# Both overflow blocks of two expert layers behind one branch at the end, and the early rows' routing between the first layer's products

## The chip, the cores and the metric

The kernel runs on one core of a Trainium2 chip. The metric is the device time of one execution in microseconds (us), lower is better. An execution is timed from outside; the profiled one also has a span, from its first to its last instruction.

## What is computed

A chunked state-space attention gives `x` of shape (3072, 256). Two mixture-of-experts layers follow, each with 8 experts, one expert per row, and no limit on how many rows an expert may get:

```python
def _moe_ref(x, expert_emb, tau, w1, w2):
    ...
    logits = xn @ en.T / tau
    expert_idx = np.argmax(logits, axis=1)
    ...
    for e in range(E):
        mask = expert_idx == e
        ...
        h = np.maximum(x[mask] @ w1[e], 0.0)
        out[mask] = gate_w[mask, None] * (h @ w2[e])
    return out.astype(np.float32)

def reference(**kwargs):
    ...
    x = _moe_ref(x=x, **moe_kwargs)
    return _moe2_ref(x=x, **moe2_kwargs)
```

`_moe2_ref` is the same with `logits = x @ w_gate`. The weights are 256x1024 and 1024x256 per expert.

## The kernel before

**Stages.** The attention runs first and routes its rows by batches: GpSimd (POOL) scatters each row with indirect DMAs into a DRAM buffer `scr1`, in which every expert of the first layer has its own stretch (`route`, L144 to L229). The first layer takes the experts in turn: SyncE (SP) loads the expert's rows (`load_rows`, L274), TensorE (PE) transposes them (`x_split_k`, L284), multiplies by the first weights in eight column blocks (`mm1_f`, L299; tiles h0 to h7), then by the second (`mm2_steps`, L321; tiles y0 and y1). Weights and rows are split into a high and a low part, so each product is three matmuls. ScalarE (ACT) and VectorE (DVE) take each h tile out of PSUM (hh on ACT at L311, then hl on DVE at L312) and split the next expert's weights between (`wsplit`, L104: a cast on ACT at L120, a difference on DVE at L121). `finish1` (L395) routes the results into `scr2`, and the second layer reads them from there and scatters its results into `out` (`put_out`, L434).

**Capacities.** The main code of the first layer takes 432 rows of an expert (NMX). That of the second takes 384 rows and, behind one branch per expert (L1322), 256 more. The branch's condition is a count that every engine loads into a register (`values_load`, a TENSOR_LOAD at L1320). Rows past these capacities go through `rest` (L460): a register load of the largest count (L465), one branch over the whole block (L467), and inside it, for each expert, another load, another branch and a loop over 128 rows. `rest(0, ...)` stands before the first layer's first expert (L1220), `rest(1, ...)` before the second layer's (L1303). With these inputs neither block is entered.

**Early rows.** 162 rows of the first expert (NE0) are there after half of the batches; `early1` (L359) multiplies them during the attention, and tile names end in m0a. Their routing into `scr2` is the generator `prev` at L1223, which is run to its end (L1224) before the first expert's other 270 rows are transposed (L1226). `early_rows` and `mm1_early` do the same for 128 rows of the first two experts of the second layer (names n0a, n1a).

**Order.** The order of instructions on each engine is the order of the code (`manual_schedule`, L57); each engine runs its own in sequence. A generator's `yield` marks where other work may be put; `adv(1)` (L1229) runs `prev` by one such step after each h tile of the first layer.

**A skipped block.** On the skipped side of a branch each engine waits for what it still has in flight on the semaphores that the block would use and raises them as the block would have; on POOL this ends in an INC_SWDGE_SEM. After the last line every engine has a DRAIN and a barrier (L1398).

Of the kernel before, what the change touches and what calls it, by code (L numbers as in the profile page):

```python
# [9 lines left out]
F32 = mybir.dt.float32  # L10
F32R = mybir.dt.float32r
BF16 = mybir.dt.bfloat16
I32 = mybir.dt.int32
AF = mybir.ActivationFunctionType
ALU = mybir.AluOpType
AX = mybir.AxisListType
PSUM = bass.MemoryType.PSUM
# [12 lines left out]
R1 = NTOK + 384  # L30
R2 = NTOK + 512
# [5 lines left out]
def ssm_moe_moe_kernel(  # L37
# [44 lines left out]
    def wload0(raw):  # L82
        """weights of the first expert"""
        for which in range(2):
            w0.append(raw[:, which * KD * F:(which + 1) * KD * F])
            sp.dma_start(w0[which], wsrc[0][which][0])
            for k in range(2):
                wraw[2 * which + k] = w0[which][:, k * WP:(k + 1) * WP]
# [55 lines left out]
    def route(pn, nt, scale, vi, which, rows, scr, scr_rows, scats, psp, tag, lag=0, hole=None):  # L144
        """rows [pn,nt,272]: values and logits, id; vi [pn,nt,2] valid, invalid. To the experts' rows of scr."""
# [85 lines left out]
    def make_hole(which, n, ne, psp, name):  # L231
        """rows to leave out so that the next row of each of the first ne experts is its n-th or a later one"""
        pr = psp.tile([128, 512], F32, tag="c", name="hole" + name)
        pe.matmul(pr[:1, :ne], lhsT=ones[:, 0:1], rhs=cums[which][:, :ne], start=True, stop=True)
        t = const.tile([1, ne], F32, name="t" + name)
        dve.tensor_scalar(t, pr[:1, :ne], -1.0, float(n), op0=ALU.mult, op1=ALU.add)
        dve.tensor_scalar(holes[which][:, :ne], t, 0.0, None, op0=ALU.max)

    def counts(cum, hole, psp, name):
        """row 0: the eight counts; then their maximum"""  # L240
        pr = psp.tile([128, 512], F32, tag="c", name="cnt" + name)
        pe.matmul(pr[:1, :E], lhsT=ones[:, 0:1], rhs=cum[:], start=True, stop=hole is None)
# [103 lines left out]
    def begin1(xr, pn, nt, tag, rows=None):  # L346
        """ids; which rows hold a token"""
        if rows is None:
            rows = xpool.tile([128, 4, 272], F32, tag="rows2", name="rows2" + tag)
            va = rt.tile([128, NT, 2], F32, tag="va", name="va" + tag)  # L350
        else:
            rows, va = rows
        pool.tensor_copy(rows[:pn, :nt, 265:266], xr[:pn, :nt, 265:266])
        pool.tensor_scalar(va[:pn, :nt, 0:1], xr[:pn, :nt, 265:266], float(NTOK), None, op0=ALU.is_lt)
        pool.tensor_scalar(va[:pn, :nt, 1:2], xr[:pn, :nt, 265:266], float(NTOK), BIG,
                           op0=ALU.is_ge, op1=ALU.mult)
        return rows, va

    def early1():  # L359
        """rows for the first expert that are there after half of the batches"""  # L360
# [99 lines left out]
    def rest(m, cnt, done, scr, base, psp):  # L460
        """rows of any expert past the first `done`, 128 at a time"""
        why = "counts of tokens"
        with tc.tile_pool(name=f"rest{m}", bufs=1) as rp:
            top = NTOK + (NE if m else NE0)
            nmax = nc.values_load(cnt[0:1, E:E + 1], min_val=0, max_val=top,  # L465
                                  skip_runtime_bounds_check_because=why)
            with tc.If(nmax > done):  # L467
                for e in range(E):
                    n = nc.values_load(cnt[0:1, e:e + 1], min_val=0, max_val=top,
                                       skip_runtime_bounds_check_because=why)  # L470
                    with tc.If(n > done):
                        ws = []
                        for which in range(2):
                            w = rp.tile([128, KD * F], F32, tag=f"w{which}", name=f"rw{m}_{e}_{which}")
                            sp.dma_start(w, wsrc[m][which][e])
                            ws.append(w)
                        sp.dma_start(scr[ds(e * base + n, 128), :], zrow[:, 0, :])
                        with tc.For_i(done, n, 128) as i:
                            row = nc.s_assert_within(
                                i, 0, base - 128, skip_runtime_bounds_check_because=why)  # L480
                            rest_block(m, rp, psp, scr[ds(e * base + row, 128), :], ws, f"r{m}_{e}")

    def rest_block(m, rp, psp, src, ws, tag):
# [15 lines left out]
        if m == 0:  # L499
            yt = rp.tile([128, KD, 128], F32, tag="yt", name="yt" + tag)  # L500
            for dd in range(KD):
                p = psp.tile([128, 512], F32, tag="a", name=f"y{dd}{tag}")
                for f in range(KF):
                    o = f * D + dd * 128
                    pe.matmul(p[:, :128], lhsT=ws[1][:, o:o + 128], rhs=ht[:, f, :],
                              start=(f == 0), stop=(f == KF - 1))
                act.copy(yt[:, dd, :], p[:, :128])
            for _ in finish1(yt, xr, begin1(xr, 128, 1, tag), 128, 1, psp, None, tag):
                pass
        else:  # L510
            ids = out_rows(xr, 128, 1, tag)
            p = psp.tile([128, 512], F32, tag="a", name=f"o{tag}")
            for f in range(KF):
                pe.matmul(p[:, :D], lhsT=ht[:, f, :], rhs=ws[1][:, f * D:(f + 1) * D],
                          start=(f == 0), stop=(f == KF - 1))
            put_out(p, xr, ids, 128, 0, False, tag)

# [1 line left out]
    scats1 = []  # L519
    with ExitStack() as actx:  # L520
# [11 lines left out]
        def load_half(n):  # L532
            """B^T and C^T of half the chunks of a batch, all heads"""
# [10 lines left out]
        def expand_half(n, raw):  # L544
            """block diagonal over the two heads of a unit"""
# [50 lines left out]
        def cb_steps(b, k):  # L596
            """C B^T of chunks 2k, 2k+1 of all heads, times L"""
# [52 lines left out]
        def expand_x(q, xc, copy=dve.tensor_copy):  # L650
            """block diagonal over the two heads"""
# [9 lines left out]
        def dma_x(q):  # L661
            """the same without an engine"""
# [11 lines left out]
        def quad_p(q):  # L674
            """decays from the start of a chunk, on the partitions of its C"""
# [12 lines left out]
        def quad_c(q, r):  # L688
            """decayed C, block diagonal over the chunks of a group"""
# [9 lines left out]
        # chunk c of a quad: bank ((c - 1) // 4) % 3, slot (c - 1) % 4  # L699
# [58 lines left out]
        # token tiles of a batch in the order in which they become ready  # L758
# [41 lines left out]
        def run(gen, n=None):  # L800
            """advance gen by n steps (to its end if n is None)"""
# [33 lines left out]
        # idk[p, k] = [p mod 32 = k]; hm[p, h] = [p // 16 mod 2 = h]  # L835
# [14 lines left out]
        def a_part(lo, hi):  # L850
            """decays in parts hi (rows 0:32) + lo (rows 32:64), 0 at the start of a chunk"""
# [32 lines left out]
        def chunk_start():  # L884
            """decays from the start of a chunk; decays of whole chunks"""
# [17 lines left out]
            # on the partitions (4 heads, d)  # L903
# [271 lines left out]
    with ExitStack() as c1:  # L1175
# [44 lines left out]
        rest(0, cnt1, NMX, scr1, R1, psM)  # L1220
# [3 lines left out]
        for _ in prev:  # L1224
            pass
# [43 lines left out]
        # rows for the first experts of the second layer that are there already  # L1269
# [28 lines left out]
    N2, X2 = C2P * C2T, C2P * X2T  # L1298
    psM = ctx.enter_context(tc.tile_pool(name="psM2", bufs=2, space=PSUM))
    psX = ctx.enter_context(tc.tile_pool(name="psX", bufs=3, space=PSUM))  # L1300
    psH = ctx.enter_context(tc.tile_pool(name="psH2", bufs=3, space=PSUM))

    rest(1, cnt2, N2 + X2, scr2, R2, psM)  # L1303
    epool = ctx.enter_context(tc.tile_pool(name="epool", bufs=1))
    for e in range(E):
# [27 lines left out]
        xr, xs, nt = nxr, nxs, nnt  # L1333

# [5 lines left out]
def _layout(inputs):  # L1340
# [14 lines left out]
    # chunk c = 4 g + r + 1 at rows (r, h, n)  # L1355
# [46 lines left out]
```

## Time and profile before

| what | us |
|---|---|
| three executions | 504.42, 508.36, 508.38 |
| median | 508.36 |
| span of the profiled execution | 502.2 |
| median less span | 6.2 |
| PE busy in the span | 459.6 |

The page gives the profiled execution by its span alone; what lies around the span is taken as the 6.2 us of the last but one line. In the rows further down, PE is the matmuls and PEld the weight loads; a q behind an engine's name is its sequencer or queue, which executes register loads, branches and semaphore instructions, and these do not count as busy. PEclk is the granted clock of TensorE as a share of its full 2.4 GHz, so 0.50 is 1.2 GHz.

### The profile page before, as it was taken

To read this page: it belongs to the slowest core of one execution; us is meant where nothing else is said; L and a number is where in the kernel's file an instruction comes from. 1 tells how busy PE (TensorE), PEld (TensorE's weight loads), DVE (VectorE), ACT (ScalarE), POOL (GpSimd) and SP (SyncE) were. 2 spreads that over 40 slices of the span, in tenths; PEclk is the share of its full clock that TensorE was granted. 3 is DMA by queue.
4 is the path that set the end of the run, shared out by engine and by line. 5 is a ranking of instruction groups with operands and counts; after the bars stand their busy time and mean duration, and the time that the engine had idled before them with its cause. 6 is when DMAs were issued, how large, how long until landed. Compare 5 with 4: busy or idle time off the path is not lost.

```text
span 502.2 us, 8903 instructions
## 1 busy us (share of the span) xinstructions
PE 459.6 (92%) x3177; PEld 413.3 (82%) x3177; DVE 288.2 (57%) x681; ACT 240.6 (48%) x557; POOL 138.2 (28%) x210
## 2 busy tenths in 40 slices
PE   7969988888869999999999999969999999999992
PEld 3645656667769999999999999869999999999991
DVE  6786788777645836547373656723666357244330
ACT  5532454456535544637354455524566346344330
POOL 6334456165730031230303021411101210212011
PEclk9857999989879999999999999989999999999997
DMA  7265799995225534242443444260654564411000
GB/s 249 89 200 118 190 230 245 219 281 185 89 80 173 180 110 179 92 159 104 142 145 119 144 136 177 79 213 19 222 192 159 170 217 154 134 40 58 22 23 15
DMA packets 50226, 72.22 MB, mean 144 GB/s; under 512 B 23870, under 2 KB 36093, under 8 KB 49899
## 3 DMA queue, kind: packets, MB, share of 16 engines
q1 hardware_dynamic: 45595, 61.66, 40.8%
q0 software_dynamic: 4560, 9.70, 5.8%
q8 instruction: 34, 0.56, 0.5%
q14 instruction: 37, 0.30, 0.2%
HBM read 52.53 MB, written 19.74 MB: 144 GB/s over the span
## 4 chain that ended last, share of the span: by engine, by line
PE 34%; DMA 21%; issue 12%; POOL 2%; POOLq 1%; another core or an unknown queue 0%; DVE 0%; ACT 0%
DMA out_dram<-os0n,idsn 13%; PE y1m L330 7%; DMA out_dram<-os0n0a,idsn0a 7%; PE y0m L330 7%; PE h0m L308 2%; PE h1m L308 2%; PE h6m L308 2%; PE h2m L308 2%; PE h3m L308 2%; PE h5m L308 2%; PE h4m L308 2%; PE h7m L308 2%; POOL out_dram L437 1%; POOL scr L218 1%; PE rkm L197 1%
## 5 line engine op out<-in xcount | busy, mean ns | idle before, releaser
L218 POOL DMA_INDIRECT scr<-rows2m,idxm x31 | 31.5, 1017 | 126.6 <-DVE cum L215 104.1
L121 DVE TENSOR_TENSOR w0l<-raw,w0h 128x1024 fp32r<-128x1024 f32 x30 | 36.7, 1224 | 10.2 <-ACT w0h L120 10.2
L121 DVE TENSOR_TENSOR w1l<-raw,w1h 128x1024 fp32r<-128x1024 f32 x30 | 36.4, 1215 | 1.0 <-ACT w1h L120 1.0
L603 PE MATMUL cb<-cw,btt 128*128 128x256 f32 x96 | 33.1, 462 | 3.5 <-DVE mb L610 1.2
L437 POOL DMA_INDIRECT out_dram<-os0n,idsn x8 | 7.8, 971 | 88.8 <-ACT os0n L436 46.1
L218 POOL DMA_INDIRECT scr<-rows,idxa x24 | 26.1, 1086 | 22.0 <-DVE cum L215 12.3
L120 ACT CAST w1h<-raw 128x1024 fp32r<-128x1024 f32 x30 | 31.5, 1053 | 0.0
L580 DVE TENSOR_TENSOR_SCAN lt<-ab,ipat 128x512 f32<-128x512 f32 x24 | 29.2, 1216 | 3.5 <-PE ab L577 3.3
L120 ACT CAST w0h<-raw 128x1024 fp32r<-128x1024 f32 x30 | 31.1, 1041 | 0.0
L312 DVE SCALAR_TENSOR_TENSOR hln<-h0n,hhn 128x384 fp32r<-128x384 f32 (+1 forms) x8 | 4.2, 524 | 45.7 <-ACT hhn L311 45.7
L603 PEld LDWEIGHTS cb<-cw,btt 128*128 128x128 f32 x96 | 18.4, 219 | 11.2 <-issue 4.1
L610 DVE TENSOR_TENSOR mb<-cb,lt 128x256 f32<-128x256 f32 x48 | 18.0, 416 | 10.9 <-PE cb L603 10.7
L330 PE MATMUL y1m<-hhm,w1h 128*128 128x432 f32 (+1 forms) x64 | 23.0, 360 | 0.0
L330 PE MATMUL y0m<-hhm,w1h 128*128 128x432 f32 (+1 forms) x64 | 22.9, 358 | 0.0
L312 DVE SCALAR_TENSOR_TENSOR hlm<-h0m,hhm 128x432 fp32r<-128x432 f32 (+1 forms) x8 | 4.7, 586 | 31.5 <-ACT hhm L311 31.5
L330 PE MATMUL y0m<-hhm,w1l 128*128 128x432 f32 (+1 forms) x64 | 22.4, 350 | 0.0
L330 PE MATMUL y1m<-hhm,w1l 128*128 128x432 f32 (+1 forms) x64 | 22.3, 349 | 0.0
L330 PE MATMUL y0m<-hlm,w1h 128*128 128x432 f32 (+1 forms) x64 | 22.3, 348 | 0.0
L330 PE MATMUL y1m<-hlm,w1h 128*128 128x432 f32 (+1 forms) x64 | 22.3, 348 | 0.0
L704 PE MATMUL y<-mb,xbd 128*64 128x80 f32 x384 | 19.0, 246 | 2.4 <-DMA xbd<-in_xs__dram 2.0
L591 POOL TENSOR_TENSOR mb<-brt,lt 128x128 f32<-128x128 f32 x24 | 11.1, 462 | 36.8 <-DVE lt L580 30.2
L704 PEld LDWEIGHTS y<-mb,xbd 128*64 128x64 f32 x384 | 15.9, 144 | 6.0 <-issue 3.0
(603 smaller groups left out, 1552.4 us busy)
## 6 DMA issues: line engine op xcount, KB each, us to landing
raw<-in_m2w_dram SPq DMA_DIRECT2D x32, 512.0 KB
raw<-in_m1w_dram SPq DMA_DIRECT2D x28, 512.0 KB
scr<-zrow SPq DMA_DIRECT2D x8, 448.9 KB
scr<-zrow SPq DMA_DIRECT2D x8, 399.0 KB
xrm<-scr SPq DMA_DIRECT2D x7, 448.9 KB
xrn<-scr SPq DMA_DIRECT2D x6, 399.0 KB
xbd<-in_xs__dram SPq DMA_DIRECT2D x24, 96.0 KB
scr<-zrow SPq DMA_DIRECT2D x8, 266.0 KB
```

The source lines that it names most:

```text
L120: act.copy(hi[:, sl], raw)
L121: dve.tensor_tensor(lo[:, sl], raw, hi[:, sl].bitcast(F32), ALU.subtract)
L218: i = pool.indirect_dma_start(out=scr[:], out_offset=bass.IndirectOffsetOnAxis(ap=idx[:pn, t, :], axis=0), in_=rows[:, t, :W], in_offset=None,
L308: pe.matmul(p[:, :n], lhsT=w[:, o:o + 128], rhs=x[:, kd, :n], start=(k == 0), stop=(k == 5))
L312: dve.scalar_tensor_tensor(hl[:, f, :n], p[:, :n], 0.0, hh[:, f, :n].bitcast(F32), op0=ALU.max, op1=ALU.subtract,)
L330: pe.matmul(p[:, :n], lhsT=w[:, o:o + 128], rhs=h[:, f, :n], start=(k == 0), stop=(k == 3 * KF - 1))
L437: i = pool.indirect_dma_start(out=out, out_offset=bass.IndirectOffsetOnAxis(ap=ids[:pn, t, :], axis=0), in_=o[:pn], in_offset=None, bounds ...
L580: dve.tensor_tensor_scan(lts[b, g][:, 2 * v:2 * v + 2].rearrange("p u c i -> p (u c i)"), p, ipat[:].rearrange("p c i -> p (c i)"), 0.0, o ...
L591: pool.tensor_tensor(m[:, :, :, 64:80], brs[b][:, us_, 4 * g:4 * g + 4], lt[:, us_, :, CH - 1:CH].to_broadcast([128, 2, 4, NS]), ALU.mult,)
L603: pe.matmul(p[:, cc], lhsT=btt[:, c].rearrange("p h j -> p (h j)"), rhs=ctt[:, :, c * CH:(c + 1) * CH], start=True, stop=True)
L610: dve.tensor_tensor(mbs[2 * b + hq, g][:, :, o:o + 2, :64].rearrange("p u c i -> p c u i"), p[:, :, us_, :], lts[b, g][:, us_, o:o + 2, :] ...
L704: pe.matmul(yps[g][64 * hs:64 * hs + 64, r * 80:r * 80 + 80], lhsT=xts[hs][:, c, :], rhs=mbs[q, c // 4][:, hs, c % 4, :], start=(r == 0), ...
```

## The change

`rest` is taken out of both places and called once, after the second layer, with one branch for both layers' blocks. If it is entered, the first layer's block routes its rows into `scr2` past row 640 of each expert (`push_hole`), counts again, and the second layer's block follows; `scr2` gets 256 more rows per expert for this. The loop that ran the early rows' routing to its end before the first expert is gone, so that `adv(1)` runs it step by step between that expert's h tiles. The second layer's pools are closed before `rest`.

```diff
-R2 = NTOK + 512
+R2 = NTOK + 768
...
-    def rest(m, cnt, done, scr, base, psp):
+    def rest_rows(m, rp, cnt, done, scr, base, psp):
         why = "counts of tokens"
-        with tc.tile_pool(name=f"rest{m}", bufs=1) as rp:
-            top = NTOK + (NE if m else NE0)
-            nmax = nc.values_load(cnt[0:1, E:E + 1], min_val=0, max_val=top,
-                                  skip_runtime_bounds_check_because=why)
-            with tc.If(nmax > done):
-                for e in range(E):
...
+        for e in range(E):
+            n = nc.values_load(cnt[0:1, e:e + 1], min_val=0, max_val=base - 128,
+                               skip_runtime_bounds_check_because=why)
+            with tc.If(n > done):
...
+    def push_hole(n, psp):
...
+    def rest(cnt1, done1, cnt2, done2):
+        top = NTOK + NE0 + done1
+        flag = const.tile([1, 1], I32, name="flag")
+        with nc.allow_low_precision(reason="whole numbers below 2**24"):
+            dve.scalar_tensor_tensor(flag, cnt2[:, E:], float(done1 - done2), cnt1[:, E:],
+                                     op0=ALU.add, op1=ALU.max)
+        most = nc.values_load(flag[0:1, 0:1], min_val=0, max_val=top,
+                              skip_runtime_bounds_check_because="counts of tokens")
+        with tc.If(most > done1):
+            with tc.tile_pool(name="rest", bufs=1) as rp, \
+                    tc.tile_pool(name="psR", bufs=1, space=PSUM) as psr:
+                push_hole(done2, psr)
+                rest_rows(0, rp, cnt1, done1, scr1, R1, psr)
+                cnt3 = counts(cums[1], holes[1], psr, "m3")
+                rest_rows(1, rp, cnt3, done2, scr2, R2, psr)
...
         xr = load_rows(scr1[NE0:NMX, :], pn, nt, scats1, "m0")
-        rest(0, cnt1, NMX, scr1, R1, psM)
         fpool.append(c1.enter_context(tc.tile_pool(name="first", bufs=1)))
         xs = x_tiles("m0")
         prev = route(C0P, C0T, None, va0[:C0P], 1, rows0[:C0P], scr2, E * R2, scats2, psM, "m0a")
-        for _ in prev:
-            pass
         for k in range(KD):
             x_split_k(xr, pn, nt, xs, k, psM, "c", "m0")
...
-    rest(1, cnt2, N2 + X2, scr2, R2, psM)
...
         xr, xs, nt = nxr, nxs, nnt
+    ctx2.close()
+    rest(cnt1, NMX, cnt2, N2 + X2)
```

On TensorE, where the first expert begins: rk is the tile in which `route` counts rows (L197), xT0m and xT1m are the transposed rows. Before:

```order
L467 UNCONDITIONAL_BRANCH
L197 LDWEIGHTS ones
L197 MATMUL rkm0a<-cum_80,ones 81x16
L197 LDWEIGHTS ones
L197 MATMUL rkm0a<-er_75,ones 81x16
L197 LDWEIGHTS ones
L197 MATMUL rkm0a<-ohm0a,ones 81x8
L197 LDWEIGHTS tri
L197 MATMUL rkm0a<-ohm0a,tri 81x16
L289 MATMUL xT0m_2859<-ident,xrm_1772 128x90 x3
L289 MATMUL xT1m_2865<-ident,xrm_1772 128x90 x3
```

In the changed kernel the transposes stand right behind the early rows' last matmuls, and the count stands between the fifth and the sixth h tile of the first expert:

```order
L308 MATMUL h4m_1859<-xhm_1777,w0l_0_1709 128x270
L197 LDWEIGHTS ones
L197 MATMUL rkm0a<-cum_80,ones 81x16
L197 LDWEIGHTS ones
L197 MATMUL rkm0a<-er_75,ones 81x16
L197 LDWEIGHTS ones
L197 MATMUL rkm0a<-ohm0a,ones 81x8
L197 LDWEIGHTS tri
L197 MATMUL rkm0a<-ohm0a,tri 81x16
L308 MATMUL h5m_1873<-xhm_1777,w0h_0_1708 128x270
```

So the branch is gone here, and the count with its wait for ohm0a has moved behind five of the expert's eight h tiles.

On VectorE, in the same stretch of the changed kernel (before, L149 to L215 of the early rows stood ahead of xlm, all in one piece):

```order
L312 SCALAR_TENSOR_TENSOR hlm_1796<-h1m_1809,hhm_1795 128x270
L121 TENSOR_TENSOR w0l_1_1819<-raw_1339,w0h_1_1818 128x1024
L154 TENSOR_TENSOR candm0a<-rows_88,mxm0a 81x16
L157 TENSOR_TENSOR dm0a<-rows_88,mxm0a 81x16
L160 SCALAR_TENSOR_TENSOR candm0a<-candm0a,iot 81x16
L312 SCALAR_TENSOR_TENSOR hlm_1796<-h2m_1829,hhm_1795 128x270
L163 TENSOR_REDUCE mnm0a<-candm0a 81x2
L166 TENSOR_TENSOR ohm0a<-candm0a,mnm0a 81x16
L169 TENSOR_TENSOR ohm0a<-ohm0a,va_89 81x16
L312 SCALAR_TENSOR_TENSOR hlm_1796<-h3m_1845,hhm_1795 128x270
```

And on ScalarE in that stretch of the changed kernel:

```order
L311 ACTIVATE hhm_1795<-h1m_1809 128x270
L120 CAST w0h_1_1818<-raw_1339 128x1024
L159 ACTIVATE dm0a<-dm0a 81x16
L311 ACTIVATE hhm_1795<-h2m_1829 128x270
L311 ACTIVATE hhm_1795<-h3m_1845 128x270
```

The exponential of dm0a now stands ahead of hh of the third h tile, and dm0a on VectorE stands behind a weight difference of L121.

On GpSimd, at the end of the program, before:

```order
L437 DMA out_dram<-os0x_8333,idsx_8122 3072x256
L437 DMA out_dram<-os1x_8363,idsx_8122 3072x256
L1322 UNCONDITIONAL_BRANCH
L1322 ISA
L1322 UNCONDITIONAL_BRANCH
L1398 ISA
```

In the changed kernel, behind the last L1342 (the L1322 of before), with the block of `rest` and its inner branches left out at the line of dots:

```order
L497 TENSOR_LOAD flag
L499 COMPARE_AND_BRANCH
...
L466 UNCONDITIONAL_BRANCH
L499 ISA
L499 UNCONDITIONAL_BRANCH
L1420 ISA
```

A register load, a branch over the block and the skipped side's instructions (the two lines of L499 at the end) now stand between the last scatter and the end of the program.

## Rows read from the trace of the kernel before

**Rows 1.** The page, busy time: engine, busy us (share), instructions.

```profile
PE 459.6 (92%) x3177; PEld 413.3 (82%) x3177; DVE 288.2 (57%) x681; ACT 240.6 (48%) x557; POOL 138.2 (28%) x210
```

**Rows 2.** Windows: stretch, length, busy (count) by engine, PEclk, DMA share, GB/s.

```profile
134.00:142.00 8.00, 3.60 (x27) 3.18 (x25) 2.29 (x9) 1.65 (x5) 2.75 (x6) 0.89 0.26 79
180.00:312.00 132.00, 132.00 (x756) 125.08 (x755) 74.63 (x172) 68.72 (x128) 26.71 (x46) 1.00 0.40 136
328.00:345.00 17.00, 14.04 (x107) 13.87 (x106) 5.23 (x15) 5.03 (x14) 1.37 (x2) 0.90 0.51 156
```

**Rows 3.** Line L467: engine, operation, ns min/median/max, first and last start.

```profile
L467 POOLq EVENT_SEMAPHORE  x11: 17/43/1238, 137.1 to 337.6; - x11
...
L467 ACTq EVENT_SEMAPHORE  x4: 17/17/17, 140.9 to 334.0; - x4
...
L467 PEldq COMPARE_BRANCH  x2: 3607/4040/4472, 137.3 to 329.1; - x2
L467 POOLq INC_SWDGE_SEM  x2: 660/1003/1346, 137.8 to 337.7; - x2
L467 ACTq COMPARE_BRANCH  x2: 45/48/50, 138.0 to 331.3; - x2
```

**Rows 4.** Timeline, first expert: start, us, instruction [idle before]; then three windows.

```profile
136.99 0.40 PE L408 MATMUL rw1m0a<-ig,ytm0a 128*81 128x136 f32 x2
...
137.99 5.03 SPq L279 DMA_DIRECT2D xrm<-scr  x2
...
142.64 0.68 PE L289 MATMUL xT0m<-ident,xrm 90*128 90x90 f32 x3 [0.40 <-SPq L467]
...
149.26 0.28 PE L308 MATMUL h5m<-xhm,w0h 128*128 128x270 f32 x1
...
139.50:140.40 0.90, 0.00 (x0) 0.00 (x0) 0.34 (x2) 0.00 (x0) 0.00 (x0) 0.92 0.61 222
140.40:141.30 0.90, 0.00 (x0) 0.00 (x0) 0.34 (x3) 0.16 (x1) 0.00 (x0) 0.50 0.06 23
...
146.00:147.00 1.00, 1.00 (x6) 1.00 (x6) 0.44 (x1) 0.20 (x1) 0.87 (x3) 0.50 0.06 22
```

**Rows 5.** Timeline, first expert: the routing's steps and the h tiles' evacuation.

```profile
140.93 0.17 DVE L157 TENSOR_TENSOR dm0a<-rows,mxm0a 81x16 f32<-81x16 f32 x1 [1.02 <-ACTq L467]
...
141.14 0.21 ACT L159 ACTIVATE dm0a<-dm0a 81x16 f32<-81x16 f32 x1 [3.24 <-DVE dm0a L157]
141.22 0.17 DVE L163 TENSOR_REDUCE mnm0a<-candm0a 81x2 f32<-81x16 f32 x1
...
142.02 0.21 PE L197 MATMUL rkm0a<-ohm0a,tri 81*81 81x16 bf16 x1
...
148.38 0.40 ACT L311 ACTIVATE hhm<-h2m 128x270 fp32r<-128x270 f32 x1
...
149.65 0.43 DVE L312 SCALAR_TENSOR_TENSOR hlm<-h2m,hhm 128x270 fp32r<-128x270 f32 x1
```

**Rows 6.** Timeline of PE, from the early rows of the second layer to its main rows.

```profile
330.61 0.28 PE L455 MATMUL o0n1a<-w1h,hlna 128*128 128x256 f32 x1
333.85 0.36 PE L308 MATMUL h0n<-xhn,w0h 128*128 128x256 f32 x1 [2.96 <-PEq L467]
```

**Rows 7.** The end: chain that ended last; POOL's timeline; lines L1398, L1322, L1320.

```profile
490.33 2.29 DMA out_dram<-os0x,idsx
...
493.39 0.97 POOL L437 DMA_INDIRECT out_dram<-os1x,idsx  x1 [2.09 <-ACT os1x L436]
...
L1398 POOLq DRAIN  x3: 40/113/8070, 493.3 to 502.0; - x3
...
L1322 PEldq COMPARE_BRANCH  x10: 70/268/338, 345.5 to 490.1; - x10
...
L1322 POOLq INC_SWDGE_SEM  x6: 1376/1516/1767, 348.5 to 463.6; - x6
...
L1320 POOLq TENSOR_LOAD <-cnt_m x8: 290/297/302, 347.9 to 480.3; - x8
```

More of the change, by code (lines that the diff above doesn't have):

```diff
@@ L458, in mm2_out @@
             put_out(p, xr, ids, pn, t, track, tag)
-    def rest(m, cnt, done, scr, base, psp):
+    def rest_rows(m, rp, cnt, done, scr, base, psp):
         why = "counts of tokens"
-        with tc.tile_pool(name=f"rest{m}", bufs=1) as rp:
-            top = NTOK + (NE if m else NE0)
-            nmax = nc.values_load(cnt[0:1, E:E + 1], min_val=0, max_val=top,
-                                  skip_runtime_bounds_check_because=why)
-            with tc.If(nmax > done):
-                for e in range(E):
[L469 to L481, printed above, removed]
@@ new lines, in rest_rows @@
+        for e in range(E):
+            n = nc.values_load(cnt[0:1, e:e + 1], min_val=0, max_val=base - 128,
+                               skip_runtime_bounds_check_because=why)
+            with tc.If(n > done):
+                ws = []
+                for which in range(2):
+                    w = rp.tile([128, KD * F], F32, tag=f"w{which}", name=f"rw{m}_{e}_{which}")
+                    sp.dma_start(w, wsrc[m][which][e])
+                    ws.append(w)
+                sp.dma_start(scr[ds(e * base + n, 128), :], zrow[:, 0, :])
+                with tc.For_i(done, n, 128) as i:
+                    row = nc.s_assert_within(
+                        i, 0, base - 128, skip_runtime_bounds_check_because=why)
+                    rest_block(m, rp, psp, scr[ds(e * base + row, 128), :], ws, f"r{m}_{e}")
@@ new lines, in push_hole @@
+    def push_hole(n, psp):
+        pr = psp.tile([128, 512], F32, tag="c", name="holer")
+        pe.matmul(pr[:1, :E], lhsT=ones[:, 0:1], rhs=cums[1], start=True, stop=True)
+        t = const.tile([1, E], F32, name="tr")
+        d = const.tile([1, E], F32, name="dr")
+        dve.tensor_scalar(t, pr[:1, :E], -1.0, float(n), op0=ALU.mult, op1=ALU.add)
+        dve.tensor_scalar(t, t, 0.0, None, op0=ALU.max)
+        dve.tensor_copy(holes[1], t)
+        dve.tensor_tensor(d, t, holes[1], ALU.subtract)
+        dve.tensor_tensor(cums[1][0:1], cums[1][0:1], d, ALU.add)
@@ L507, in rest_block @@
                 act.copy(yt[:, dd, :], p[:, :128])
-            for _ in finish1(yt, xr, begin1(xr, 128, 1, tag), 128, 1, psp, None, tag):
+            for _ in finish1(yt, xr, begin1(xr, 128, 1, tag), 128, 1, psp, None, tag, holes[1]):
                 pass
@@ L1298, in ssm_moe_moe_kernel @@
     N2, X2 = C2P * C2T, C2P * X2T
-    psM = ctx.enter_context(tc.tile_pool(name="psM2", bufs=2, space=PSUM))
-    psX = ctx.enter_context(tc.tile_pool(name="psX", bufs=3, space=PSUM))
-    psH = ctx.enter_context(tc.tile_pool(name="psH2", bufs=3, space=PSUM))
-    rest(1, cnt2, N2 + X2, scr2, R2, psM)
-    epool = ctx.enter_context(tc.tile_pool(name="epool", bufs=1))
+    ctx2 = ctx.enter_context(ExitStack())
+    psM = ctx2.enter_context(tc.tile_pool(name="psM2", bufs=2, space=PSUM))
+    psX = ctx2.enter_context(tc.tile_pool(name="psX", bufs=3, space=PSUM))
+    psH = ctx2.enter_context(tc.tile_pool(name="psH2", bufs=3, space=PSUM))
+    epool = ctx2.enter_context(tc.tile_pool(name="epool", bufs=1))
     for e in range(E):
```

## The prediction

> **What bounds the kernel now.** I read the page's busy times first, then the windows by stage, then the places where the change cuts: the line of the skipped branch, the timeline of the first expert, the timeline of PE before the second layer, and the end. PE is busy in 459.6 of 502.2 us [rows 1], and in 180 to 312 us it is busy without a break at full clock [rows 2]. A reader should take from this that the kernel can gain only where PE stands still or is granted half its clock, and in the tail after PE's last product. Two of those places are the skipped blocks: 134 to 142 us holds 3.60 us of PE work in 8, and 328 to 345 holds 14.04 in 17, both at less than the full clock [rows 2]. The branch itself shows why. On PE it takes 3607 ns in the first place and 4472 ns in the second [rows 3]. ACT's branch is over in 50 ns, but its next instruction stands 2.9 us later (138.0 to 140.9), and in the second place 2.7 us later (331.3 to 334.0) [rows 3]. So every engine pays about 3 to 4 us to get to the other side of the long block, within the branch or behind it.
>
> The profiled span is 502.2 us. The median of the runs is 508.36, 6.2 us more. I reckon against the span and add the 6.2 at the end.
>
> **First place: the branch goes, the count moves.** PE's last early product starts at 136.99 and lasts 0.40; the first transpose xT0m starts at 142.64, held by SP's end of the block [rows 4]. Without the branch the transpose waits for its data alone. The load of these rows is issued at 137.99; in 139.50 to 140.40 the DMA engines are 61% busy at 222 GB/s, and from 140.40 on only 6% at 23 [rows 4]. The data is there by 140.4, its semaphore not later than 142.24, where SP let xT0m go (0.40 before its start). I take the middle, 141.3, so the transposes start 1.3 us earlier (2.2 to 0.4). That is far less than the 5.25 us that the gap shows: what is late next is the load, which the branch had hidden.
>
> The removed loop ran the routing of the early rows inside that gap. Now its steps stand among the h tiles. The matmuls of rk, whose last ones wait for ohm0a, stand on PE between h4 and h5, and PE runs in order, so h5 to h7 and all behind them queue behind that wait. The chain to it in the order after: candm0a and dm0a stand on VectorE behind the weight difference that, before, ended where hl of h2 starts, at 149.65 [rows 5]. From there two small steps of 0.17 (0.34), the exponential on ACT 0.21, behind it hh of h2 0.40, then on VectorE hl of h2 0.43, then from mnm0a to the last matmul of rk 0.80 (141.22 to 142.02) [rows 5]. The sum is 2.18, so rk's last matmul comes at 151.8 and h5 at about 151.9; before, h5 started at 149.26 [rows 4]. That is a stall of 2.6 us. It shifts with the start, so it is counted apart from the 1.3. It is 0 at the least, if VectorE gets to the small steps early, and 2.8 at the most with 0.2 for the two further rk matmuls.
>
> The clock: PE is granted 0.50 from 140.4, 3 us after it fell idle, and is still at 0.50 in 146 to 147 [rows 4]. After the change PE is idle for about as long without rk's matmuls, so I count the same loss: 0. A bound on the good side is 1.2 us, if the half clock ended at its old time though the work starts earlier. On the bad side the stall of 2.6 us may make it fall again. The nearest row is the second place, where an idle time of 2.96 costs 1.7 (next part).
>
> Net of the first place: −1.3 + 2.6 = **+1.3 us**, with bounds −2.5 (no stall) and +4.
>
> The other steps of the route are priced at nothing. Its scatters on POOL move from about 144 to 154; the only reader of `scr2` near is the second layer, far behind. SP's next row loads come a few us earlier because SP no longer waits. VectorE's small steps are the same ones, laid into a stage where it has 43% to spare (57% busy [rows 1]); if that cover is missing, it is the stall just counted. `push_hole`, `rest_rows` and the larger `scr2` move nothing, since the block is not entered.
>
> **Second place.** Between the last early matmul (330.61) and h0n (333.85) PE stands 2.96 us for L467 [rows 6]. Nothing else waits there: the rows of the main part were loaded before. I count 333.85 − 330.61 less a matmul's spacing of 0.12, the 2.96 and a little: 3.1 us. Then the clock: the stretch 328 to 345 has a mean of 0.90 [rows 2], so 17 × 0.10 = 1.7 us of it is lost to the half clock that follows the gap. With no gap I expect no fall. Net **−4.8 us**; if the rows or weights of the first expert are the next wait, it is less, and I keep −3.1 as the other end.
>
> **The tail.** Before, the last scatter os1x is issued on POOL at 493.39, and the one ahead of it takes 2.29 us to land [rows 7], so it lands at about 495.7. POOL's DRAIN of L1398 starts at 493.3 and lasts 8.07 us to 501.4 [rows 7]. The program ends with it. After the change POOL has these steps behind the scatter and ahead of the DRAIN: a register load of the flag 0.3 (L1320's 297 ns [rows 7]), a branch 0.05, the way to the far side 2.9 (ACT's, above), its semaphore steps, 43 ns in the median and 1238 at the most [rows 3], for which I estimate 0.6 in all, and an INC_SWDGE_SEM. That one grows over the run: 660 and 1346 ns [rows 3], then 1767 at the most [rows 7]; I take 1.8. The sum, 0.3 + 0.05 + 2.9 + 0.6 + 1.8, is 5.65, so the DRAIN starts at about 499.0 instead of 493.3.
>
> How long is a DRAIN that starts when everything has landed? No row shows one. From both sides: if it needs its 8.07 whole, the end moves by 5.7; if its length were a fixed end of the program's own, the move would be hidden, 0. The nearest row is this DRAIN itself: 5.7 us of it lie behind the landing (501.4 − 495.7). I take those: 499.0 + 5.7 = 504.7, **+3.3 us**.
>
> A page of the Trainium skill speaks of the branch: "Runtime: NRT & Kernel Launch", section "Instruction fetch mechanics", says that a taken branch whose target lies outside the current pages forces a fetch of the target before execution goes on. PE's 3607 and 4472 ns on L467 [rows 3] agree with it, and the 70 to 338 ns of the near branches of L1322 [rows 7] do too. "Advanced Engine Details and Errata", section "Control Flow Timing", gives about 108 ns for a compare-and-branch; by that alone the 2.9 us at the end would be 0.1, the tail +0.5 and the time 505.4 instead of 508.2. The rows of L467 speak against it for a block of this length.
>
> **The sum.** +1.3 − 4.8 + 3.3 = −0.2 us. Against the median that is 508.36 − 0.2 = **508.2 us**: what the second place gives, the tail and the stall take back.
>
> **Rivals.**
> - *The tail is hidden* (B). DRAIN has work of its own that can start only from the scatters' end, and the register load, the fetch and INC fit beside it, so that the program ends as before. For it: DRAIN lasts 8.07 us now, longer than the 5.7 that are added. Against: POOL executes in order, and the DRAIN stands behind these steps. Then 1.3 − 4.8 = −3.5: 504.9 us.
> - *The DRAIN takes its 8.07 us whole wherever it starts* (C, slower than before). Place: POOL, behind the last scatter. Price +5.7, so 1.3 − 4.8 + 5.7 = +2.2: 510.6 us. For it: POOL's other DRAINs, 40 and 113 ns [rows 7], show that the long one is no mere wait for landed scatters, which take 2.3. Against: part of it lies beside a transfer now. It decides from a tail over 3.5 us, where the sum of the other two is used up.
> - *No stall in the first layer* (D). VectorE has the steps of the route done before PE reaches rk. For it: VectorE has idle time; against: the order puts dm0a behind a weight difference and its exponential ahead of hh of h2. First place −1.3, sum −1.3 − 4.8 + 3.3 = −2.8: 505.6 us.
> - B and D together give 508.36 − 6.1 = 502.3; C with a second fall of the clock behind the stall gives 512.3.
>
> **How the numbers follow.** Chances: my forecast 0.42, the hidden tail 0.25, the whole DRAIN 0.20, no stall 0.13, the two combinations within B and C. The range 503.0 to 512.0 takes in all four and the likely part of the combinations. About 1% (5.1 us) is what a measurement of this kernel can tell from no change, that is under 503.3 or over 513.4. Under 503.3 lies only B with D or with the best ends of the bounds: 0.13. Over 513.4 lies only C with the clock's fall and a worse end of the first place: 0.07. The rest, 0.80, is within 1%.
>
> **What would show it.** In the profile of the changed kernel: xT0m at about 141.3, behind the load and no branch; if it starts at 138, the landing was misjudged. An idle time of PE of about 2.6 us ahead of rk or h5, released by ohm0a; if there is none, D holds. h0n directly behind o0n1a, and no slice of half clock there; a wait in that place for rows or weights would make the second place wrong. POOL's DRAIN about 5.7 us behind the last scatter, 5.7 long; 8 long means C, an end of the span no later than 8 us behind that scatter means B. An INC_SWDGE_SEM of about 1.8 us ahead of it. The forecast as a whole is wrong if the second place gives less than 3 us or the tail costs more than its 8.07 us again.

## The result, and the profile after

| what | before | after |
|---|---|---|
| median of 7 runs each, us | 508.38 | 511.56 |
| ratio of after to before | | 1.0065 (95%: 1.0036 to 1.0095) |
| span of the profiled execution | 502.2 | 508.2 |
| time of that execution | | 509.98 |

The changed kernel is slower by 0.65%, some 3.3 us, and the interval does not hold 1; the forecast was 508.2 us and no change. On another chip the same comparison gave 1.0129 (1.0094 to 1.0164), so the loss is 3 to 7 us.

The profiled execution of after has 1.8 us around its span (509.98 − 508.2). So the 6.2 us by which the median before stood over the span was not time around it: that profile shows one of the shorter executions. Below, durations are therefore counted from the issue of the first expert's row load to the end, which leaves out the attention. In the profile shown of before that stretch is 364.2 us, in after 369.6.

The first place in after, by the timelines of PE and SP and two windows of PE (columns as in [rows 2], [rows 4]):

```profile
135.05 0.40 PE L408 MATMUL rw1m0a<-ig,ytm0a 128*81 128x136 f32 x2
...
138.57 0.76 SPq L279 DMA_DIRECT2D xrm<-scr  x2
...
141.84 0.68 PE L289 MATMUL xT0m<-ident,xrm 90*128 90x90 f32 x3 [6.40 <-DMA xrm<-scr]
...
150.76 0.17 PE L197 MATMUL rkm0a<-ohm0a,ones 81*81 81x8 bf16 x1 [1.70 <-DVE ohm0a L169]
...
150.82 0.37 PE L308 MATMUL h5m<-xhm,w0h 128*128 128x270 f32 x1
...
142.00:147.00 5.00, 4.93 (x22) 4.47 (x22) 1.53 (x5) 1.77 (x5) 0.69 (x3) 0.51 0.05 19
147.00:148.70 1.70, 1.70 (x16) 1.70 (x15) 1.21 (x2) 0.73 (x1) 0.00 (x0) 1.00 0.00 0
```

xT0m is held by the load alone now and starts 3.27 us after the load's issue (before: 142.64 − 137.99 = 4.65 [rows 4]). In its place PE stands 1.70 us ahead of rk's third product, released by ohm0a, and h5m follows. The half clock lasts to 147, as before.

The second place in after, PE's timeline and one window:

```profile
334.46 0.28 PE L455 MATMUL o0n1a<-w1h,hlna 128*128 128x256 f32 x1
334.58 0.28 PE L308 MATMUL h0n<-xhn,w0h 128*128 128x256 f32 x1
...
328.00:345.00 17.00, 17.00 (x147) 17.00 (x147) 8.18 (x20) 7.85 (x20) 2.51 (x3) 1.00 0.54 167
```

Where [rows 6] had 2.96 us of idle time, h0n stands one spacing of 0.12 behind o0n1a, and the stretch that [rows 2] had at 0.90 of the clock has 17.00 of 17 us at 1.00.

The end of after: the chain's step for os0x, POOL's timeline, then the lines L1420 and L499:

```profile
489.72 3.85 DMA out_dram<-os0x,idsx
...
494.34 0.98 POOL L437 DMA_INDIRECT out_dram<-os1x,idsx  x1 [3.64 <-DMA out_dram<-os0x,idsx]
...
L1420 POOLq DRAIN  x3: 40/107/7023, 500.3 to 507.9; - x3
...
L499 POOLq EVENT_SEMAPHORE  x6: 17/30/43, 497.9 to 498.3; - x6
...
L499 PEldq COMPARE_BRANCH  x1: 3900/3900/3900, 490.1 to 490.1; - x1
...
L499 POOLq COMPARE_BRANCH  x1: 45/45/45, 494.6 to 494.6; - x1
L499 POOLq INC_SWDGE_SEM  x1: 1873/1873/1873, 498.4 to 498.4; - x1
```

Three things differ from [rows 7]. os0x takes 3.85 us to land instead of 2.29, and the last scatter, which waits for it, starts 4.62 us behind it instead of 3.06. POOL's branch at 494.6 has its next step at 497.9. The DRAIN starts 6.0 us behind the last scatter's start, not with it, and lasts 7.02 us instead of 8.07.

Where the time went, worked out from the starts in the trace: between the named instructions, in us. The second column of each kernel is from a second profile (the runs b0_before_again and a0_after_again, below).

| stretch | before | | after | | difference | forecast |
|---|---|---|---|---|---|---|
| load's issue to y0m (first place) | 13.88 | 13.35 | 14.96 | 15.36 | +1.1, +2.0 | +1.3 |
| y0m to xT0n | 175.58 | 176.06 | 177.80 | 176.35 | +2.2, +0.3 | 0 |
| xT0n to h4n (second place) | 10.84 | 8.81 | 6.10 | 6.11 | −4.7, −2.7 | −4.8 |
| h4n to issue of os0x | 152.04 | 152.38 | 152.29 | 152.92 | +0.3, +0.5 | 0 |
| issue of os0x to the end (tail) | 11.85 | 11.85 | 18.40 | 18.54 | +6.6, +6.7 | +3.3 |
| sum | 364.19 | 362.45 | 369.55 | 369.28 | +5.4, +6.8 | −0.2 |

The second and third stretch have to be read together, for the clock's sake. In the first profile of before TensorE's clock is at half behind h0n, 334.8 to 338.2 us. In the first profile of after, the second of after and the second of before (the lines below, in this order) it is at half ahead of h0n, in the stretch from y0m to xT0n:

```profile
320.00:328.00 8.00, 7.38 (x51) 7.16 (x51) 5.00 (x28) 2.59 (x11) 3.95 (x4) 0.79 0.19 55
...
320.00:336.00 16.00, 14.97 (x107) 14.12 (x107) 10.71 (x56) 6.22 (x22) 8.75 (x10) 0.89 0.19 58
...
324.00:341.00 17.00, 13.99 (x108) 13.48 (x107) 8.88 (x35) 6.47 (x18) 5.95 (x6) 0.90 0.37 96
```

Each of them loses 1.7 us of full clock (8 × 0.21, 16 × 0.11, 17 × 0.10), as much as [rows 2] show behind h0n. So the second place's −4.7 holds a loss of clock that the changed kernel has as well, only earlier. From y0m to h4n, with the fall inside in all four profiles, after is 2.5 and 2.4 us shorter than before, not 4.7.

### The profile page after: what moved, and what is told of

Its sections match the earlier page's. It is cut to its first block, busy times and chain, and to the rows that moved or that the text cites. A ratio compares the mean times of both kernels' runs of the same rounds, so it can differ in the third digit from the quotient of the medians.

```text
span 508.2 us, 8859 instructions
## 1 busy us (share of the span) xinstructions
PE 456.7 (90%) x3177; PEld 410.7 (81%) x3177; DVE 287.1 (56%) x682; ACT 239.7 (47%) x557; POOL 138.9 (27%) x210
## 4 chain that ended last, share of the span: by engine, by line
PE 41%; DMA 23%; issue 14%; DVE 7%; POOL 3%; ACT 2%; POOLq 0%; another core or an unknown queue 0%; SPq 0%; ACTq 0%; DVEq 0%
DMA out_dram<-os0n,idsn 13%; PE y0m L330 7%; PE y1m L330 7%; DMA out_dram<-os0n0a,idsn0a 6%; PE cb L627 3%; DMA xrm<-scr 2%; POOL scr L218 2%; DVE lt L604 2%; PE h0m L308 2%; PE h6m L308 2%; PE h7m L308 2%; PE h1m L308 2%; PE h5m L308 2%; PE y L771 1%; PE h3m L308 1%
## 5 line engine op out<-in xcount | busy, mean ns | idle before, releaser
L121 DVE TENSOR_TENSOR w0l<-raw,w0h 128x1024 fp32r<-128x1024 f32 x30 | 36.7, 1224 | 10.2 <-ACT w0h L120 10.2
L121 DVE TENSOR_TENSOR w1l<-raw,w1h 128x1024 fp32r<-128x1024 f32 x30 | 36.4, 1216 | 1.0 <-ACT w1h L120 1.0
```

Of the source, the lines that this page charges most:

```text
L121: dve.tensor_tensor(lo[:, sl], raw, hi[:, sl].bitcast(F32), ALU.subtract)
```

## The experiments

The first five were to price the parts one by one. Every run has a short name in brackets, by which it is called further down.

**The kernel before again** (b0, no edit), and the **changed kernel again** (a0, no edit).

> The kernel before, once more, for a second profile. Two profiled executions (of before 502.2 us of span, of the changed kernel 508.2) differ by 6.0 us, the medians by 3.2. Theory: the profile of before caught one of its shorter executions (504.42), and the part up to the first expert accounts for the difference, so a second one has a span of 505 to 507 us with a tail from the last scatter's issue to the end of 9 us as before. Rival: the span is 502 again, and the medians hide something at the program's start.

The span was 508.2 us. The load was issued at 145.68 instead of 137.99, so the attention accounts for more than the whole 6.0 us and the rest was 1.7 us shorter. The tail was 11.85 us again. The theory held, but for the span, which came out 1 us over its range. Over all profiles of this study the load's issue lies between 138.0 and 147.6 us. Between two profiles of one kernel it differs by 7.7 us (before) and 8.8 us (after), the rest by 1.7 and 0.3: most of the variation lies ahead of the change. In this second profile the clock did not fall behind the second gap, where h0n waited 2.49 us, but had fallen earlier (the window 324 to 341 above):

```profile
341.00 0.36 PE L308 MATMUL h0n<-xhn,w0h 128*128 128x256 f32 x1 [2.49 <-PEq L467]
```

> The changed kernel once more, for a second profile and a narrower ratio. Theory: all that the change does lies behind the load of the first expert's rows, so from that load's issue to the end the second profile has 368 to 370.5 us like the first (369.55), against 362.5 and 364.2 of the kernel before, and from os0x's issue to the end 18.4; the time differs between executions by when that load is issued. Ratio to before 1.003 to 1.012. Rival: the tail's delay of os0x (3.85 instead of 2.3) was chance, the end is 16.9 from os0x's issue, and the ratio is 1.0.

Ratio 1.0129 (1.0094 to 1.0164), a median of 515.92 us beside 511.0 on that chip; just past the upper end of what was expected. From the load's issue 369.28 us, from os0x 18.54: the tail is not chance.

**Without the end block** (e1):

```diff
     ctx2.close()
-    rest(cnt1, NMX, cnt2, N2 + X2)
```

> The changed kernel without the call of rest: rows past the capacities would not be computed (there are none with these inputs). Theory: the tail costs 6.5 us in the changed kernel (1.56 for the landing of os0x that the far fetch delays, 4.95 between the last scatter's issue and DRAIN's end), so the time is 511.6 - 6.5 = 505.1, with os0x landing in 2.3 us and the DRAIN 8 us long right behind the last scatter. Rival: the DRAIN and the landing vary by themselves and the block costs only its 0.3 + 2.9 + 1.9: 506.5 to 508. Second rival: the tail is no loss, 511.

505.41 us, ratio 0.9890 (0.9837 to 0.9944). The tail is that of before, 11.87 us: os0x lands in 2.30, and the DRAIN starts behind the last scatter and lasts 8.08. The theory held; the block at the end costs 18.40 − 11.87 = 6.5 us.

**The routing drained first** (e2):

```diff
+        for _ in prev:
+            pass
         for k in range(KD):
             x_split_k(xr, pn, nt, xs, k, psM, "c", "m0")
```

> The changed kernel with the loop that runs the early rows' routing to its end put back ahead of the first transposes. Theory: the routing fits into the wait for the first expert's rows, so the stall of 1.70 ahead of rk goes, and nothing is late in its place: 511.6 - 1.7 = 509.9, down to 509.2 if the wait of 0.39 for the third row load goes too. Rival: the routing's small products delay the transposes as before and the order changes nothing: 511.6.

Ratio 1.0024 (0.9993 to 1.0056), where the changed kernel had 1.0065. From the load's issue to y0m 12.96 us instead of 14.96, with no wait ahead of rk. So the interleaving costs 2.0 us, and the routing fits into the wait for the load. The wait ahead of the third row load did not go (from y0m to its first transpose 15.97 us, 15.46 in the changed kernel), so that part of the expectation fell. To the end of the program 1.2 to 1.5 us of the 2.0 are left: PE now waits 2.19 us for the second layer's first rows (xT0n).

**Before, without the second block** (e3):

```diff
-    rest(1, cnt2, N2 + X2, scr2, R2, psM)
```

> The kernel before without the call of rest(1) ahead of the second layer, nothing else changed: rows past the second layer's capacity would not be computed (there are none). Theory: this place is worth the gap of 3.1 and the 1.7 of half clock behind it: 508.4 - 4.8 = 503.6, with h0n right behind o0n1a at full clock. Rival: the gap closes, but rows or weights are late next, or the clock falls anyway: 505.3 to 507.

507.83 us, ratio 0.9942 (0.9909 to 0.9974), 2.9 us less. From the load's issue 359.42 us, 4.8 less than in the first profile of before and 3.0 less than in the second. From o0n1a to h0n it is 3.24 us in the first and 2.77 in the second, and 0.12 here. The 1.5 of half clock (h0n to h4n 4.44 us, 2.90 in the second profile) is only in the first. With the gap closed another wait showed, 0.48 us for VectorE ahead of h3n. From y0m to h4n this run is 4.1 and 2.5 us shorter than the two profiles of before. The theory's place was right and its price was that of one execution.

The next three take the tail apart. The first two edit the end block of the changed kernel: only one expert of the second layer in it (e5), and one instruction in it (e6). The third leaves out scatters (e7).

```diff
-        for e in range(E):
+        for e in range(E - 1, E):
...
-                push_hole(done2, psr)
-                rest_rows(0, rp, cnt1, done1, scr1, R1, psr)
-                cnt3 = counts(cums[1], holes[1], psr, "m3")
-                rest_rows(1, rp, cnt3, done2, scr2, R2, psr)
+                rest_rows(1, rp, cnt2, done2, scr2, R2, psr)
```

> The changed kernel with an end block that holds the last expert of the second layer only (rows past the capacities of the others, and of the first layer, would not be computed; there are none). The flag, the branch and POOL's INC stay, the block is about a tenth as long. Theory: the far side is then near, so no engine fetches it: os0x lands in 2.3 us instead of 3.85, POOL gets from the branch to the DRAIN in 2.4 us instead of 5.7, and the DRAIN takes its 7 again. Issue of os0x to the end is 11.9 without a block and 18.4 with the long one; here about 13.5 to 14.0, the time 511.6 - 4.6 = 507. Rival: what costs is the waiting and the INC, and the length of the block is no matter: 18 us, 511.

From os0x to the end 13.52 us; os0x landed in 2.30, the DRAIN started 2.46 us behind the last scatter's start. Ratio 0.9999 (0.9961 to 1.0036), 510.82 us on a chip where before had 511.72: the time expected, 507, was missed, the tail was as expected. The lines of L499 and of the DRAIN in this run:

```profile
L499 PEldq COMPARE_BRANCH  x1: 220/220/220, 498.3 to 498.3; - x1
...
L499 POOLq COMPARE_BRANCH  x1: 45/45/45, 501.3 to 501.3; - x1
L499 POOLq EVENT_SEMAPHORE  x1: 17/17/17, 501.4 to 501.4; - x1
L499 POOLq INC_SWDGE_SEM  x1: 1835/1835/1835, 501.5 to 501.5; - x1
...
L1417 POOLq DRAIN  x3: 40/107/7023, 503.4 to 511.0; - x3
```

POOL's next step stands 0.1 us behind its branch instead of 3.2, and PE's branch takes 220 ns instead of 3900.

```diff
         with tc.If(most > done1):
-            with tc.tile_pool(name="rest", bufs=1) as rp, \
...
-                rest_rows(1, rp, cnt3, done2, scr2, R2, psr)
+            dve.memset(flag, 0)
```

> The changed kernel with an end block of one VectorE instruction (rows past the capacities would not be computed; there are none). The flag, its five register loads and the branch stay; POOL has nothing to raise for the block. Theory: register load 0.3 and branch 0.05 are all that is left, and the DRAIN, which lasts at least 7 us from its start and 5.7 from the last landing, is as long as without a block: issue of os0x to the end 12.0 to 12.3, time 505.5. Rival: the DRAIN takes long because it starts behind a branch at all, and the tail stays at 13.5 or more.

```profile
L1415 POOLq DRAIN  x3: 40/113/7535, 498.5 to 506.6; - x3
```

From os0x to the end 11.87 us, as without a block, though the DRAIN starts 0.5 us later: it lasts 7.54. Ratio 0.9927 (0.9880 to 0.9974), 508.65 us on a chip that gave before 511.72. The register load and the branch are hidden; the theory held for the tail.

```diff
+    def pt_skip(tag):
+        return tag in ("n0", "n1", "n2", "n3", "n4", "n5", "n6")
+
     def put_out(p, xr, ids, pn, t, track, tag):
...
+        if track and pt_skip(tag):
+            return
         i = pool.indirect_dma_start(
...
-    rest(cnt1, NMX, cnt2, N2 + X2)
```

> The changed kernel without the end block, and without the scatters of the main rows of the second layer's experts 0 to 6 (their rows of the output are not written: 21 scatters fewer of 85). Theory: the DRAIN's 8.07 us is work per scatter that POOL has issued, so it takes 8.07 x 64/85 = 6.1 us. Rival: it is a fixed time of the program's end or of the last scatters, and stays at 8.07.

```profile
L1424 POOLq DRAIN  x3: 40/113/6528, 498.1 to 505.2; - x3
```

6.53 us, shorter by 1.54: it is not fixed, so the rival fell. The trace has 66 scatters instead of 85, so 19 were left out and not 21, and each is worth 81 ns. What looks like a fixed rest is the last scatter itself. By the starts in the trace the DRAIN begins 0.07 us ahead of it, and POOL executes it for 0.97 us; the DRAIN's remainder is 7.03 us for 85 scatters and 5.48 for 66, 83 ns each in both. So the theory held, counted from the last scatter's end. It rests on one run with another count.

**Near blocks.** What e5 showed was tried on whole kernels: the blocks' eight unrolled experts as one loop, in the places of before (first, g1) and at the end, with the routing drained (second, g2). The edit of the first:

```diff
-                for e in range(E):
-                    n = nc.values_load(cnt[0:1, e:e + 1], min_val=0, max_val=top,
+                with tc.For_i(0, E, 1) as ev:
+                    e = nc.s_assert_within(ev, 0, E - 1, skip_runtime_bounds_check_because=why)
+                    n = nc.values_load(cnt[0:1, ds(e, 1)], min_val=0, max_val=top,
...
-                            sp.dma_start(w, wsrc[m][which][e])
+                            sp.dma_start(w, wsrc[m][which][ds(e, 1)].rearrange("a p f -> (a p) f"))
...
```

> The kernel before with both blocks in their old places, their eight unrolled experts written as one loop over the expert, so that each block is about an eighth as long; the function is the same. Theory: what PE pays for a skipped block is the fetch of a far target, so L467 on PE falls from 3.6 and 4.5 us to 0.1 to 0.4 as at the near branches, h0n follows o0n1a within 1 us instead of 3.2, the clock has less cause to fall there, and nothing is added at the end (11.9 us from os0x's issue): 3 to 4.5 us less than before, ratio 0.991 to 0.994. Rival: PE's long branch is a wait for the count or for the other engines, the block's length is no matter: ratio 1.0 and L467 on PE at 4 us again.

506.32 us beside 510.36, ratio 0.9928 (0.9900 to 0.9956): 0.7% less than before, where the changed kernel had 0.65% more. Line L467 and PE's timeline, to be read beside [rows 3] and [rows 6]:

```profile
L467 PEldq COMPARE_BRANCH  x2: 212/296/379, 142.6 to 334.6; - x2
L467 POOLq INC_SWDGE_SEM  x2: 643/984/1325, 143.6 to 337.9; - x2
...
336.75 0.36 PE L308 MATMUL h0n<-xhn,w0h 128*128 128x256 f32 x1 [0.30 <-PEq L467]
```

PE's branches fall from 3607 and 4472 ns to 212 and 379, and the wait ahead of h0n from 2.96 us to 0.30. With these inputs the loop is not entered; what it costs when it is was not tried.

> The changed kernel with the early rows' routing run to its end ahead of the first transposes, and the end block's experts written as loops, so that its far side is near; the function is the changed kernel's. Theory: first place as in the run with the routing drained (13.0 us from the load's issue to y0m), second place without a gap, and the tail of the short block, 13.5 us from os0x's issue to the end instead of 18.4: 511.6 - 2.0 - 4.9 = 504.7, ratio to before 0.99 to 0.995. Rival: two loops of POOL's and SP's instructions are still too long for the near side, the tail stays over 17 and the ratio at 1.0.

Ratio 0.9977 (0.9933 to 1.0020), 511.1 us beside 510.36: the gain expected did not come whole. The first place took 13.92 us, with a longer stretch of half clock, and from os0x to the end it took 15.57 us, not 13.5: POOL's far step was gone (the DRAIN started 2.93 us behind the last scatter's start), but os0x still took 4.07 us to land. The trace lists the fetches of instructions as transfers of their own. Here one of 16 KB starts 1.52 us behind os0x's issue, in the changed kernel one at 1.42, both about 1 us behind PE's branch; in the runs with a landing of 2.3 none of 16 KB falls between the issue and the landing. The views of the DMA engines show what that does. First the changed kernel from 489.7 to 494.0, in 40 slices of 0.11 us, with its queues, then the run with the short block from 497.8 to 502.0, both from just ahead of os0x's issue:

```profile
DMA  0000000000100796510000010200000020000000
...
q0 software_dynamic: 48, 0.09, 6.3%
q14 instruction: 3, 0.02, 2.2%
q8 instruction: 1, 0.02, 2.0%
```

```profile
DMA  0000000000000007880000000000000000000001
...
q0 software_dynamic: 48, 0.09, 6.4%
q14 instruction: 1, 0.01, 0.5%
```

The software queue q0 carries the 48 packets of os0x, the queues q8 and q14 the fetches. By the starts in the trace all 48 begin within 0.4 us in the short block's run. In the changed kernel 41 of them do; the other seven begin up to 1.3 us later, beside one fetch of 16 KB and three of 8. In g2 that one of 16 KB is the only fetch from os0x's issue to the last of its packets, three packets begin late, and PE's branch takes 428 ns: the landing is late without a long branch on PE. The last run (h1) was to move the fetch of 16 KB.

```diff
+        pw = psM.tile([128, 512], F32, tag="c", name="fill")
+        for k in range(40):
+            pe.matmul(pw[:, :128], lhsT=ones[:], rhs=ones[:], start=True, stop=True)
```

> The run with the routing drained and rolled blocks, and 40 products of a constant with itself on TensorE, into a tile that nothing reads, while it waits for the first expert's rows; they move TensorE's later instructions by 80 places in its program. Theory: os0x lands late because TensorE's fetch of 16 KB of instructions falls 1.5 us behind its issue; 80 places later in the program it does not fall there, so os0x lands in 2.3 us, from its issue to the end are 13.5 us instead of 15.6, and the time falls by 1.5 to 2. Rival: any block at the end delays the landing (the register loads and the branch on the other engines do), and the landing stays at 4. Beside this, TensorE is not idle in the wait, so its clock may stay at full speed through the first h tiles: 4.0 to 4.5 us from h0m to h4m instead of 5.8.

Ratio 0.9952 (0.9917 to 0.9988), but the landing did not change: the last scatter started 4.56 us behind os0x, and the fetch came 1.44 us behind it as before. So it does not sit at a place of the program that chance moved there; in all five profiles that have it, it starts 1.0 to 1.1 us behind PE's branch. And the same block was near for PE in g2 and far here:

```profile
L500 PEldq COMPARE_BRANCH  x1: 3695/3695/3695, 494.6 to 494.6; - x1
```

(428 ns in g2). h0m to h4m took 5.82 us, as in g2: the filling products, from 143.8 to 147.2 us, did not hold the clock, which was granted at 1.00 to 145 and at 0.51 in 145 to 148. The rival, that any block delays the landing, is spoken against by e5 and e6, whose landings are 2.3 behind the same register loads and branches.

## Why the prediction was wrong, point by point

- **First place, +1.3.** Right: +1.1 in the pair of profiles that it was made on. The load's wait (xT0m at 141.3 for an issue at 137.99, so 3.3 us) measured 3.27; the stall of 2.6 measured as 2.07 of h4m to h5m above the 0.74 of before (the wait itself 1.70). e2 shows it is the interleaving, 2.0 us. One thing was not seen: in the second profile of before the first transposes start 3.48 us after the load's issue though the branch is there, since the load is issued late enough for the branch to be over. So the 1.3 won at the start is there in one execution and not in the other, where the first place cost 2.0.
- **Second place, −4.8.** Right for the gap, wrong for the clock. The gap is 3.1 us in one profile of before and 2.65 in the other, and it closes wherever the branch is gone (after, e3). The step "with no gap I expect no fall" failed: the changed kernel has no gap and loses the 1.7 us all the same, at 321 to 324 us instead of behind h0n. From y0m to h4n the gain is 2.5 and 2.4 us, and less than 3 was one of the signs that the prediction had named for being wrong.
- **Tail, +3.3.** This is the term that was mis-sized most: it measured +6.6, and e1 gives 6.5 for the block alone. Its start was right: 5.7 us later was forecast, counted from the last scatter's start it is 6.0. Two steps failed. The DRAIN was taken to last 5.7 us, what lay behind the last landing; it lasts 7.02, in e5 and in the changed kernel alike. The landing has no part in it: in all twelve profiles with 85 scatters the DRAIN ends 7.02 or 7.03 us behind the end of POOL's last scatter or behind its own start, whichever is later. And the landing of os0x was taken as 2.29 us unchanged; it is 3.85, 1.56 more, and between 3.8 and 4.1 in every run in which 16 KB of instructions are fetched in that time. The prediction named the fetch for POOL and forgot what the other engines' fetches meet on the DMA engines.
- **The sum.** With 6.6 in place of 3.3 it is +3.1, close to the measured +3.3, but that is luck in part. Of the first pair's +5.4 from the load's issue the parts are +1.1, −2.5 (from y0m to h4n), +0.3 and +6.6: the second place gave 2.3 less than forecast, and something of about 2 us ahead of the load made up for it in the medians.
- **The tail in parts, from runs:** register load and branch 0 (e6, 11.87); INC and its semaphore steps 1.7 (e5, 13.52); far side of the block 4.9 (18.40), of which 1.56 is the landing and most of the rest POOL's 3.2 us from its branch to the next step.
- **Rivals.** B, the hidden tail, holds for an empty block only (e6): a delay is hidden as long as POOL would still be executing the last scatter, about 1 us. C was the nearer one: the DRAIN comes whole but for that microsecond, and the kernel ended on the side that C named. D fell: the stall is there in every profile with the interleaving.
- **The branch rule.** The Trainium skill, "Runtime: NRT & Kernel Launch", section "Instruction fetch mechanics", says that a taken branch to a target outside the current pages has to wait for a fetch of it, and the trace bore it out: 3900 against 220 ns on PE for a long and a short block behind the same condition, and 428 against 3695 for the same block in two places. The Trainium skill's 108 ns of "Advanced Engine Details and Errata", section "Control Flow Timing", is of the size of PE's near branches (70 to 456 ns) and of none of its far ones; on POOL and ACT the branch itself takes 37 to 58 ns, near or far, and what is paid stands behind it.
- **Left open.** From the load's issue the two kernels are 5 to 7 us apart, the medians of the first comparison 3.2 and of the second 4.9; what the attention gives back in the first was not found. In after's first profile y0m to xT0n is 2.2 us longer than in before's: the clock's 1.7 and a wait ahead of rk at the layer's end of 1.79 us (0.9 in all others) make up most of it. Why the clock falls there in one run and not in the next, no run settles; in each of the 13 profiles either it falls there (after, a0, b0, e1, e5, g2, h1) or PE waits 0.8 to 2.2 us for the rows of xT0n (before, e2, e3, e6, e7, g1), never both. That the fetch delays os0x was seen in every run with a fetch there (after, a0, e2, g2, h1) and not in the others, but no run moved the fetch alone.

## What to carry to other kernels

A skipped block is paid for by its length and its place in the program, on every engine that must get past it: write it short (a loop instead of unrolled experts) before looking for another place for it. The end of the program is not a free place: the engine that ends it pays the way past the block in full, and what it delays there (a scatter, the DRAIN) as well. A loss of clock that one profile shows behind a gap is not won by closing the gap: a second profile of the same kernel shows whether the two belong together. And steps that fit into a wait that is there anyway cost nothing; spread over busy products they can cost a stall, which the order of every engine behind them shows.

## What had not been expected

- POOL's DRAIN at the end lasts 7.02 us where nothing is under way any more (e5, after), and counted from the last scatter's end just as long where it follows at once: 83 ns for each scatter of the program (e7).
- POOL's INC_SWDGE_SEM grows in the same way, by about 22 ns for each scatter issued so far, on the average: 1346 ns behind 59 of them, 1767 behind 80 (before), 1873 behind 85 (after).
- One and the same skipped block is passed on PE in 428 ns or in 3695; between the two kernels only 40 products ahead of it differ (g2, h1).
- Five engines pass the block at different times, and the transfer that suffers, os0x's rows, was issued by POOL, which reaches its own branch only after they have landed (4.9 us behind the issue against 3.85).
